# A spectral mixer and a gated FFN on one core: the head between them written in another order

## The chip, the cores and the metric

The kernel runs on one core of a Trainium2 chip. Its engines are TensorE (PE in the profile, PEld for its weight loads), VectorE (DVE), ScalarE (ACT), GpSimd (POOL) and SyncE (SP, which issues the DMAs here). Each has a queue of its own and runs it in order; an instruction that waits holds up what stands behind it on its engine. The metric is the device time of one execution in microseconds. The kernel before takes 500.88 us, the median of 3 runs (500.87 to 501.19).

## The reference

```
def _A_ref(x, w_r, w_i):                       # x: [1, 2048, 576]
    X = rfft2(x.astype(float32), axes=(-2, -1))
    X = X * (w_r + 1j * w_i)
    return irfft2(X, s=(S, D)).astype(bfloat16)

def _B_ref(x, w_gate, w_up, w_down):           # 576 -> 4608 -> 576
    return (_gelu(x @ w_gate) * (x @ w_up)) @ w_down

x = A_x
h = x + _A_ref(_layernorm(x, axis=-1), A_w_r, A_w_i)
out = h + _B_ref(_layernorm(h, axis=-1), B_w_gate, B_w_up, B_w_down)
```

Inputs and output are bfloat16. `_layernorm` subtracts a row's mean and divides by the root of its variance plus 1e-5, and `_gelu` is the tanh form.

## The kernel before

The 2048 rows lie in 16 tiles of 128 rows, `h_sb[:, h]`, and the two transforms are matrix products split into factors (16 by 128 along the rows).

**The spectral part** (to about 59 us). Rows are normalised and transformed in groups of 16 (`row16`), and then a loop runs over the eight entries of `order` = 1, 2, ... 7, 0. Iteration i does the column transform of entry i (`f2`, copied from PSUM by `f2_out`, L489), the 128-point transform of entry i - 1 (`f3`, copied at L514), VectorE's complex multiplication with the weights (`wmul`, L543 to L575) and the inverse 128-point transform of an older entry (`i3`, products at L592 and L616, copies into `EO` at L600 to L629). `EO[0]` and `EO[1]` hold the two halves x = 0 and 1 of the inverse; the last entry, 0, belongs to x = 1.

**Column products.** `inv_cols(x, g)` is the inverse column transform of half x for the pair of row tiles 2g and 2g + 1: ten matmuls into one PSUM tile (`cs_ps`, L643), then its copy. For g = 0 and 1 the copy gives two bfloat16 tiles `cs` (L666 on ScalarE, and for x = 1 one of the two at L664 on VectorE); for g of 2 and more one float32 tile `cw` on ScalarE (L656). This text calls them product (x, g) and copy (x, g).

**The head** (L843 to L867, about 60 to 73 us) brings the first four row tiles into the form that the FFN reads. `add_rows(g)` forms the inverse 16-point transform in two PSUM tiles (`y_ps`, L764, 16 matmuls), the y pair of row tiles 2g and 2g + 1. `add_sum(h)` adds one of them to `h_sb` on VectorE, with the row's sum read out behind it (L809), and has ScalarE square the result for the row's sum of squares (L817). `head_rstd(h)` makes variance and mean of it by three small VectorE instructions (L822, L825, L826) and the reciprocal root on POOL (L827). `norm_row(h)` normalises the row (L136); `turn(h)` transposes it by 18 TensorE instructions (L836) and VectorE copies the result into `hl` (L837). Tiles 0 and 1 go that way. Tiles 2 and 3 are normalised in a doubled form (`norm2`, L789) and transposed by a DMA from SP (`flip`, L801). `load_wd(2)` stands behind them on SP.

**The FFN.** `gate(t, f, ...)` computes 128 of the 4608 gate and up columns for a block of up to 512 rows: 18 matmuls into one PSUM tile (`gu`, L890), GELU on ScalarE (L898) and the multiplication on VectorE (L899), which is the last reader of the PSUM tile. Since tiles 0 and 1 are ready first, the first six gates run on 256 rows alone, and the column products that remain stand between them. After them come the main gates, 36 per block of four row tiles, with the rest of the row tiles' sums, statistics and rows put between them by a table (`todo`: `fold`, `add_both`, `stats2`, `norm2`, `flip`), and after each block the down products (`acc`, L926 and L945) and the output.

**Order and PSUM.** The whole runs under `tc.manual_schedule()`: each engine's instructions come in the order in which the text issues them. All PSUM tiles of these stages have one tag with four buffers, the whole of PSUM:

```
def two(name):
    return psum.tile([P, 2, 512], FP32, name=name, tag="two", bufs=4)
```

So a product whose tile is the fifth waits until the last reader of an earlier tile is done. In the head of before, the written order is: products (0,0) to (0,2), the last but one `i3`, (0,3), (0,4), the last `i3`, (0,5), (1,0), (1,1), both y pairs, sums 0 and 1, (0,6), sum 2, (0,7), rstd 0, sum 3, rstd 1, rows 0 and 1, (1,2), (1,3), both transposes, and rstd, row and flip of tiles 2 and 3; and products (1,4) to (1,7) stand behind the second to fifth of the six half gates.

Of the kernel before, what the change touches and what calls it, by code (L numbers as in the profile page):

```python
# [9 lines left out]
ACT = mybir.ActivationFunctionType  # L10
ALU = mybir.AluOpType
FP32 = mybir.dt.float32
# [8 lines left out]
P = 128  # L21
# [5 lines left out]
JP = J + 1  # L27
# [14 lines left out]
def kernel_body(  # L42
# [13 lines left out]
    A = nc.scalar  # L56
# [4 lines left out]
    keep = ctx.enter_context(tc.tile_pool(name="keep", bufs=1))  # L61
# [4 lines left out]
    def two(name):  # L66
        return psum.tile([P, 2, 512], FP32, name=name, tag="two", bufs=4)
# [8 lines left out]
    def const(name, val):  # L76
        t = keep.tile([P, 1], FP32, name=name)
        V.memset(t[:], val)
        return t

    zerob = const("zerob", 0.0)
# [166 lines left out]
    def angle_c(sl):  # L248
        drop_sign(ab[:, sl], ab[:, sl])
# [4 lines left out]
    def cosine(sl):  # L254
        A.activation(TF[:, sl, 1, :], ab[:, sl], ACT.Sin, bias=nhpib[:], scale=2.0 * PI / S)

    def minus_sine(sl):
        V.tensor_scalar(TF[:, sl, 0, :], TF[:, sl, 2, :], -1.0, None, op0=ALU.mult)

    def turn_tf(sl):  # L260
        nc.sync.dma_start(
            TI[:, sl].rearrange("p k r q -> p (k r) q"), TF[:, sl].rearrange("p k r q -> p (k r q)"), transpose=True
        )
# [200 lines left out]
    order = [1, 2, 3, 4, 5, 6, 7, 0]  # L464
# [6 lines left out]
    def f2(c):  # L471
        ps = two("pq_ps")
        col = slice(slot[c] * P, (slot[c] + 1) * P)
        steps = [(par, t) for par in range(2) for t in (par, par + 2, 4)]
        if c == order[0]:
            steps.sort(key=lambda s: s[1] == 4)
        for par, t in steps:
            T.matmul(  # L478
                ps[:, par, 0:JP],
                lhsT=Bt[:, t, col],  # L480
                rhs=DT[:, t // 2, par] if t < 4 else DF[:, par],
                start=(t == par),
                stop=(t == 4),
            )
        pq[c] = wk.tile([P, 2, JP], BF16, name="pq", tag="pq", bufs=6)
        pq_ps[c] = ps

    def f2_out(c, copy=A.copy, rs=slice(0, 2)):
        copy(  # L489
            pq[c][:, rs].rearrange("p r (j a) -> p r j a", a=2),  # L490
            pq_ps[c][:, :, 0:JP].rearrange("p a (r j) -> p r j a", r=2)[:, rs],
        )
# [27 lines left out]
    def sums_of(k):  # L520
        g, hs = gk[k], hk[k]
        x = xab[k] = wk.tile([P, 2, 2, JP], BF16, name="xab", tag="xab", bufs=2)
        V.tensor_tensor(x[:, 0, :, 0:J], g[:, :, 0:J], hs[:, :, 0:J], ALU.subtract)
        V.tensor_tensor(x[:, 1, ::-1, 0:J], g[:, :, 0:J], hs[:, :, 0:J], ALU.add)
# [109 lines left out]
    cs = {}  # L634
    cw = {}

    def inv_cols(x, g):

        ps = two("cs_ps")
        for w in range(NW):  # L640
            for e in range(2):
                rows = slice(64 * e, 64 * e + JW)
                T.matmul(  # L643
                    ps[:, e, 0:JP],
                    lhsT=EO[x][rows, w, 2 * g : 2 * g + 2].rearrange("p h e k l -> p (h e k l)"),
                    rhs=DQ[rows, w] if w or e else DT[rows, 0, :, 0, :],
                    start=(w == 0),
                    stop=(w == NW - 1),
                )
        pv = ps[:, :, 0:JP].rearrange("p t (q a) -> p t q a", q=2)  # L650
        if g >= 2:
            if x == 0 or g == 2:
                cw[x, g] = eop.tile([P, 2, JP], FP32, name=f"cw{x}{g}")[:]
            else:
                cw[x, g] = cwb[:, g - 3]
            A.activation(  # L656
                cw[x, g].rearrange("p t (a q) -> p t q a", q=2), pv, ACT.Copy, scale=Y_SCALE
            )
            return
        ts = [eop.tile([P, JP], BF16, name=f"cs{x}{g}{t}") for t in range(2)]  # L660
        for t in range(2):
            dst = ts[t][:].rearrange("p (a q) -> p q a", q=2)
            if x == 1 and t == 1:
                V.tensor_scalar(dst, pv[:, t], Y_SCALE, None, op0=ALU.mult)  # L664
            else:
                A.activation(dst, pv[:, t], ACT.Copy, scale=Y_SCALE)  # L666
        cs[x, g] = ts
# [4 lines left out]
    for i in range(n + 1):  # L672
        last = i >= n
        if not last:
            f2(order[i])
            if i != 1:
                f2_out(order[i])
        if i == 0:
            f2(order[0] + 8)
            for r in range(2):  # L680
                f2_out(order[0] + 8, V.tensor_copy, slice(r, r + 1))
            angle_c(rest)
            minus_sine(rest)

        if 1 <= i <= n:
            f3(order[i - 1], 0)
            f3(order[i - 1], 1)
            if i == 1:
                f2_out(order[1])
                sums_of(order[0])  # L690
            else:
                if i == 2:
                    cosine(rest)
                    turn_tf(rest)
                    pre = [load_gu(g) for g in range(3)]
                    nc.sync.dma_start(wd_a[:], wd_view[:, 0:NWA, :])
                wmul(order[i - 2], i - 1, order[i - 1])
        if not last and i:
            f2(order[i] + 8)
            f2_out(order[i] + 8)  # L700
        if i >= 3:
            for s in range(3):
                i3(order[i - 3], s)
        if last:
            wmul(order[i - 1], i)
        if i == 1:
            scr_pool.__exit__(None, None, None)
            eop = ctx.enter_context(tc.tile_pool(name="eop", bufs=1, side="right"))
            EO = [eop.tile([P, 5, H, 2, 4, 8], BF16, name=f"EO{x}", tag=f"EO{x}") for x in range(2)]
    for g in (0, 1, 2):  # L710
        inv_cols(0, g)
    for s in range(3):
        i3(order[6], s)
    for g in (3, 4):
        inv_cols(0, g)
    for s in range(3):
        i3(order[7], s)
    inv_cols(0, 5)

    spw.__exit__(None, None, None)  # L720
    spec.__exit__(None, None, None)
# [32 lines left out]
    def add_rows(g):  # L754


        ys = [two("y_ps") for _ in range(2)]
        sl = (slice(0, DH), slice(DH, 0, -1))
        for b in range(2):
            steps = [(x, t) for x in range(2) for t in range(2 if g < 2 else 1)]  # L760
            for s, (x, t) in enumerate(steps):
                for i in range(2):
                    rows = slice(64 * i, 64 * i + 64)
                    T.matmul(  # L764
                        ys[i][:, b, 0:DH],
                        lhsT=G16[rows, b * t, x, :],
                        rhs=cs[x, g][t][rows, sl[b]] if g < 2 else both[x, g][rows, b, :],
                        start=(s == 0),
                        stop=(s == len(steps) - 1),
                    )  # L770
        return ys
# [33 lines left out]
    def add_sum(h, ys, squares=True):  # L805


        hv = h_sb[:, h, :].rearrange("p (b n) -> p b n", b=2)
        V.scalar_tensor_tensor(  # L809
            hv, ys[h % 2][:, :, 0:DH], 1.0, hv, op0=ALU.mult, op1=ALU.add, accum_out=sums[:, h, 0:1]  # L810
        )
        if squares:
            sum_squares(h)
# [5 lines left out]
    def head_rstd(h):  # L819


        V.scalar_tensor_tensor(  # L822
            mv2[:, h, 1:2], sums[:, h, 0:1], sums[:, h, 0:1], sums[:, h, 1:2], op0=ALU.mult, op1=ALU.subtract
        )
        V.tensor_scalar(rstd2[:, h : h + 1], mv2[:, h, 1:2], -1.0 / (D * D), 1e-5, op0=ALU.mult, op1=ALU.add)  # L825
        V.tensor_scalar(mv2[:, h, 0:1], sums[:, h, 0:1], 1.0 / D, None, op0=ALU.mult)  # L826
        G.tensor_tensor(rstd2[:, h : h + 1], rstd2[:, h : h + 1], mhalf[:, h : h + 1], ALU.pow)  # L827

    def turn(h):


        q = h % 4 * P
        pt = psum.tile([P, 2048], BF16, name="pt", tag="two", bufs=4)
        for r in range(NR):
            for p0 in (0, 64):
                T.transpose(pt[p0 : p0 + 64, r * P : (r + 1) * P], ln2[h][:, r * 64 : (r + 1) * 64], ident[:])  # L836
        V.tensor_copy(hl[0][:, :, q : q + P], pt[:, 0 : NR * P].rearrange("p (r q) -> p r q", q=P))  # L837
# [4 lines left out]

    inv_cols(1, 0)  # L843
    inv_cols(1, 1)
    y0 = add_rows(0)
    y1 = add_rows(1)
    add_sum(0, y0)
    add_sum(1, y0)
    inv_cols(0, 6)
    add_sum(2, y1)  # L850
    inv_cols(0, 7)
    head_rstd(0)
    add_sum(3, y1)
    head_rstd(1)
    norm_row(0)
    norm_row(1)
    inv_cols(1, 2)
    inv_cols(1, 3)
    turn(0)
    turn(1)  # L860
    head_rstd(2)
    norm2(2)
    flip(2)
# [34 lines left out]
        A.activation(g_sb, gu[:, 0, 0:n], ACT.Gelu_apprx_tanh)  # L898
        V.tensor_tensor(p_sb(f)[:, lo:hi], g_sb, gu[:, 1, 0:n], ALU.mult)  # L899

    late = [(1, g) for g in range(4, 8)]
    for f in range(2 * FQ):
        gate(0, f, groups[f // FQ], f % FQ, 0, 2 * P)
        if f and late:
# [100 lines left out]
```

## Time and profile before

| | |
|---|---|
| median of 3 runs | 500.88 us |
| the profiled execution | 500.97 us |
| its span in the trace | 499.1 us |
| instructions | 12531 |
| PE busy | 488.1 us (98%) |
| DVE busy | 222.4 us (45%) |
| ACT busy | 162.7 us (33%) |
| POOL busy | 29.0 us (6%) |
| granted TensorE clock | full in all of the 40 slices |

Times are microseconds from the start of the span, mean durations nanoseconds. A row of the timeline gives start, duration, engine, line, operation, what it writes and reads, its shape, how many were merged, and in brackets the idle time of the engine ahead of it with what ended that. Merged rows overlap a little. TensorE's instructions are pipelined, so a row's end lies behind the start of the next one, and "PE busy" is not TensorE at its peak. The chain of waits is followed back from the last instruction and gives, for each stretch of time, the work that everything behind it waited for.

### The profile page before, as it was taken

The numbers are of one execution on the slowest core, as the hardware profiler recorded it, in microseconds if no ns is written. First come the engines' busy times: TensorE is split into PE (matmuls) and PEld (weight loads), VectorE is DVE, ScalarE is ACT, GpSimd is POOL, SyncE is SP. The second block draws the span as 40 slices with busy tenths as digits, with TensorE's granted clock in tenths as the row PEclk, the third lists the DMA queues.
The fourth block names the chain that finished last, engine by engine and source line by source line (L and its number), as shares of the span: only waits on it lengthen the run. The fifth ranks groups of instructions, "written<-read, shape, count | busy, mean of one in ns | idle before, by whom it ended". The sixth has DMA issues, their size and how long they took to land.

```text
span 499.1 us, 12531 instructions
## 1 busy us (share of the span) xinstructions
PE 488.1 (98%) x5606; PEld 341.8 (68%) x5608; DVE 222.4 (45%) x439; ACT 162.7 (33%) x289; POOL 29.0 (6%) x78
## 2 busy tenths in 40 slices
PE   6999989999999999999999999999999999999997
PEld 3567778555579975555599955555799655555995
DVE  8989776788641235433311245333211333333111
ACT  8989874223310112323200132332110223233000
POOL 8500010011110000000000000000000000000000
PEclk9999999999999999999999999999999999999999
DMA  9739659789960019977630069876600276760000
GB/s 289 216 62 222 192 147 246 158 171 198 175 145 13 3 49 195 207 163 159 155 75 3 1 156 209 182 159 151 143 3 1 74 159 159 157 146 1 14 13 25
DMA packets 89469, 62.33 MB, mean 125 GB/s; under 512 B 23110, under 2 KB 88006, under 8 KB 89414
## 3 DMA queue, kind: packets, MB, share of 16 engines
q1 hardware_dynamic: 89126, 60.34, 54.1%
q0 software_dynamic: 288, 1.18, 0.8%
q8 instruction: 44, 0.72, 0.6%
q14 instruction: 11, 0.09, 0.1%
HBM read 52.65 MB, written 2.36 MB: 110 GB/s over the span
## 4 chain that ended last, share of the span: by engine, by line
PE 90%; DVE 2%; ACT 1%; POOL 0%; issue 0%
PE gu L890 55%; PE acc L926 27%; PE acc L945 2%; PE eo_ps L592 2%; PE cs_ps L643 1%; PE pq_ps L478 1%; PE y_ps L764 1%; DVE h_sb L809 1%; PE gh_ps L495 0%; PE gh_ps L496 0%; POOL rstd L827 0%; PE eo_ps L616 0%; DVE hrow L789 0%; DVE Bt L837 0%; PE pt L836 0%
## 5 line engine op out<-in xcount | busy, mean ns | idle before, releaser
L890 PE MATMUL gu<-Bt,wgu 64*128 64x512 bf16 (+1 forms) x2700 | 282.4, 367 | 0.9 <-DVE mv L822 0.9
L890 PEld LDWEIGHTS <-wgu 64*128 64x128 bf16 x2700 | 159.6, 94 | 119.7 <-issue 1.1
L899 DVE TENSOR_TENSOR P_sb<-g_sb,gu 128x512 bf16<-128x512 f32 (+1 forms) x150 | 99.4, 664 | 146.0 <-ACT g_sb L898 146.0
L898 ACT ACTIVATE g_sb<-gu 128x512 f32<-128x512 f32 (+1 forms) x150 | 87.0, 580 | 194.6 <-PE gu L890 194.6
L926 PEld LDWEIGHTS <-P_sb 64*128 64x128 bf16 x2160 | 128.5, 94 | 4.5
L926 PE MATMUL acc<-wd,P_sb 64*128 64x288 bf16 x1440 | 91.0, 283 | 0.0
L935 DVE TENSOR_TENSOR part<-part,acc 128x576 f32<-128x576 f32 x15 | 11.3, 754 | 111.6 <-ACT part L934 111.6
L934 ACT COPY part<-acc 128x576 f32<-128x576 f32 x15 | 9.6, 639 | 122.8 <-PE acc L926 122.8
L926 PE MATMUL acc<-wd_a,P_sb 64*128 64x288 bf16 x720 | 46.9, 283 | 0.0
L789 DVE TENSOR_SCALAR hrow<-h_sb,mv,rstd 128x1152 bf16<-128x1152 bf16 x14 | 12.1, 868 | 1.2 <-POOL rstd L827 1.2
L478 PE MATMUL pq_ps<-DT,Bt 128*128 128x290 bf16 x64 | 12.3, 286 | 0.0
L285 PE MATMUL f2t<-h_sb,ident 128*128 128x512 bf16 x26 | 8.0, 459 | 3.7 <-DMA h_sb<-in_A_x_dram 3.6
L643 PE MATMUL cs_ps<-DQ,EO 58*128 58x290 bf16 x144 | 11.6, 283 | 0.0
L937 DVE TENSOR_TENSOR h_sb<-h_sb,part 128x576 bf16<-128x576 bf16 x15 | 11.4, 757 | 0.5
L133 POOL TENSOR_TENSOR rstd<-rstd,mhalf 128x1 f32<-128x1 f32 (+1 forms) x16 | 11.4, 714 | 1.3
L478 PEld LDWEIGHTS <-Bt 128*128 128x128 bf16 x96 | 9.2, 97 | 2.5
L297 PE MATMUL f2t<-F,xn 128*128 128x256 bf16 x64 | 9.2, 275 | 1.1 <-DVE xn L136 1.1
L643 PEld LDWEIGHTS <-EO 58*128 58x128 bf16 x160 | 8.2, 94 | 2.8 <-issue 1.1
L132 POOL TENSOR_SCALAR rstd<-mv 128x1 f32<-128x1 f32 (+1 forms) x16 | 3.9, 241 | 103.7 <-DVE mv L118 103.5
L489 ACT CAST pq<-pq_ps 128x580 bf16<-128x580 f32 x15 | 9.6, 668 | 0.0
L123 ACT ACTIVATE junk<-h_sb 128x576 bf16<-128x576 bf16 x14 | 9.4, 677 | 0.4 <-DMA h_sb<-in_A_x_dram 0.4
L117 DVE BATCH_NORM_STATS2 st<-h_sb 128x6 f32<-128x288 bf16 x21 | 9.3, 442 | 0.0
(132 smaller groups left out, 265.0 us busy)
## 6 DMA issues: line engine op xcount, KB each, us to landing
wgu<-in_B_w_gate_dram SPq DMA_DIRECT2D x48, 432.0 KB
wgu<-in_B_w_up_dram SPq DMA_DIRECT2D x48, 432.0 KB
wd<-in_B_w_down_dram SPq DMA_DIRECT2D x2, 1728.0 KB
wd_a<-in_B_w_down_dram SPq DMA_DIRECT2D x1, 1728.0 KB
out_dram<-h_sb SPq DMA_DIRECT2D x3, 576.0 KB
h_sb<-in_A_x_dram SPq DMA_DIRECT2D x4, 288.0 KB
h_sb<-in_A_x_dram SPq DMA_DIRECT2D x2, 576.0 KB
WR<-in_A_w_r_dram SPq DMA_DIRECT2D x1, 650.2 KB
```

The source lines that it names most:

```text
L133: G.tensor_tensor(dst[:, sl], dst[:, sl], mhalf[:, sl], ALU.pow)
L478: T.matmul(ps[:, par, 0:JP], lhsT=Bt[:, t, col], rhs=DT[:, t // 2, par] if t < 4 else DF[:, par], start=(t == par), stop=(t == 4),)
L592: T.matmul(pv[:, n], lhsT=z[:, a, w].rearrange("p b j -> p (b j)"), rhs=TI[:, ts[k], 1 - a : 3 - a, :], start=(a == 0), stop=(a == 1),)
L643: T.matmul(ps[:, e, 0:JP], lhsT=EO[x][rows, w, 2 * g : 2 * g + 2].rearrange("p h e k l -> p (h e k l)"), rhs=DQ[rows, w] if w or e else DT ...
L789: V.tensor_scalar(hrow[:], h_sb[:, h, :].rearrange("p (r k) -> p r k", k=64).unsqueeze(2).to_broadcast([P, NR, 2, 64]), mv2[:, h, 0:1], rs ...
L890: T.matmul(gu[:, c, 0:n], lhsT=w[rows, r, i * P : (i + 1) * P], rhs=hl[tcnk % 2][rows, r, lo:hi], start=(r == 0), stop=(r == NR - 1),)
L898: A.activation(g_sb, gu[:, 0, 0:n], ACT.Gelu_apprx_tanh)
L899: V.tensor_tensor(p_sb(f)[:, lo:hi], g_sb, gu[:, 1, 0:n], ALU.mult)
L926: T.matmul(accs[i][:, c, 0:DH], lhsT=p_sb(f)[rows, st * P : (st + 1) * P], rhs=wd[f // NWA][rows, f % NWA, c * DH : (c + 1) * DH], start=( ...
L935: V.tensor_tensor(part, part, accs[1][:, :, 0:DH], ALU.add)
L937: V.tensor_tensor(hv, hv, part, ALU.add)
L945: T.matmul(acc[:, 0, 0:DH], lhsT=p_sb(f)[:, st * P : (st + 1) * P], rhs=wd[f // NWA][:, f % NWA, cc], start=(f == 0), stop=(f == NFT - 1),)
```

## The change

Four edits to the order, and no change to what is computed.

- `inv_cols` is split into its matmuls (`inv_mm`) and its copy (`inv_out`), so that they can be issued apart.
- In the spectral loop the copy of entry order[1] (`f2_out`) is issued straight behind its product, ahead of the two `f3` copies of order[0], as for all other entries.
- Product (0,5) leaves its place ahead of the head. In the head a one-column GELU is issued on ScalarE behind the copies of (1,1), so that the GELU table is loaded there. The first y pair is followed by the products (0,5) and (0,6), then the second y pair; sums 0 and 1; the copies of (0,5) and (0,6); product (0,7); rstd 0 and 1, rows 0 and 1, the copy of (0,7), both transposes with their copies; then (1,2), sums 2 and 3, and tiles 2 and 3 as before.
- Product (1,3) leaves the head for the list that stands between the half gates, which then holds (1,3) to (1,7), behind the second to sixth.

```
+    inv_ps = {}
     def inv_cols(x, g):
-        ps = two("cs_ps")
+        inv_mm(x, g)
+        inv_out(x, g)
+
+    def inv_mm(x, g):
+        ps = inv_ps[x, g] = two("cs_ps")
         for w in range(NW):
...
-        pv = ps[:, :, 0:JP].rearrange("p t (q a) -> p t q a", q=2)
+
+    def inv_out(x, g):
+        pv = inv_ps[x, g][:, :, 0:JP].rearrange("p t (q a) -> p t q a", q=2)
...
             f2(order[i])
-            if i != 1:
-                f2_out(order[i])
+            f2_out(order[i])
...
             f3(order[i - 1], 1)
             if i == 1:
-                f2_out(order[1])
                 sums_of(order[0])
...
     for s in range(3):
         i3(order[7], s)
-    inv_cols(0, 5)
...
     inv_cols(1, 0)
     inv_cols(1, 1)
+    A.activation(keep.tile([P, 1], FP32, name="first_gelu")[:], zerob[:], ACT.Gelu_apprx_tanh)
     y0 = add_rows(0)
+    inv_mm(0, 5)
+    inv_mm(0, 6)
     y1 = add_rows(1)
     add_sum(0, y0)
     add_sum(1, y0)
-    inv_cols(0, 6)
-    add_sum(2, y1)
-    inv_cols(0, 7)
+    inv_out(0, 5)
+    inv_out(0, 6)
+    inv_mm(0, 7)
     head_rstd(0)
-    add_sum(3, y1)
     head_rstd(1)
     norm_row(0)
     norm_row(1)
-    inv_cols(1, 2)
-    inv_cols(1, 3)
+    inv_out(0, 7)
     turn(0)
     turn(1)
+    inv_cols(1, 2)
+    add_sum(2, y1)
+    add_sum(3, y1)
     head_rstd(2)
     norm2(2)
     flip(2)
...
-    late = [(1, g) for g in range(4, 8)]
+    late = [(1, g) for g in range(3, 8)]
     for f in range(2 * FQ):
         gate(0, f, groups[f // FQ], f % FQ, 0, 2 * P)
         if f and late:
```

## The prediction

> **What bounds the kernel now.** I read the page's first, second and fourth parts, then the chain of waits over the stretch that the change edits (about 59 to 77 us), then the timeline of all engines there. The page says that TensorE is busy nearly all the time and carries the chain:
>
> ```profile
> PE 488.1 (98%) x5606; PEld 341.8 (68%) x5608; DVE 222.4 (45%) x439; ACT 162.7 (33%) x289; POOL 29.0 (6%) x78
> ...
> PE 90%; DVE 2%; ACT 1%; POOL 0%; issue 0%
> ```
>
> After 74 us no wait of a matmul is listed at all, so whatever TensorE loses or gains before then passes to the end unchanged. Between 59 and 74 us the chain leaves TensorE (start, duration, engine, tile, line):
>
> ```profile
> 62.26 2.11 DVE h_sb L809 x6
> ...
> 67.07 0.71 PE pt L836 x18
> ...
> 67.80 0.76 DVE Bt L837
> 68.56 0.14 DVE mv L822
> ...
> 72.19 0.42 DVE P_sb L899
> ```
>
> That is: sums of tiles 0 to 2, the second row's transposes, its copy, and then not gate 0, whose matmuls follow at 68.71, but VectorE's rows of tiles 2 and 3, behind which the first multiply (L899) stands. The timeline shows who waits for that multiply:
>
> ```profile
> 63.05 0.68 ACT L817 ACTIVATE junk<-h_sb 128x576 bf16<-128x576 bf16 x1 [1.56 <-DVE h_sb L809]
> ...
> 65.47 0.28 PE L643 MATMUL cs_ps<-DT,EO 58*128 58x290 bf16 x1 [0.25 <-DVE h_sb L809]
> ...
> 68.14 1.28 ACT L898 ACT_TABLE_LOAD   x1
> ...
> 71.51 0.71 ACT L656 ACTIVATE cwb<-cs_ps 128x580 f32<-128x580 f32 x1 [0.24 <-PE cs_ps L643]
> ...
> 72.19 1.15 DVE L899 TENSOR_TENSOR P_sb<-g_sb,gu 128x256 bf16<-128x256 f32 x3
> ...
> 72.65 0.28 PE L643 MATMUL cs_ps<-DT,EO 58*128 58x290 bf16 x1 [0.19 <-DVE P_sb L899]
> ```
>
> There are four PSUM tiles. When TensorE came to the product (1,5) (72.65) they had held gates 0, 1, 2 and (1,4); (1,4) was copied out by 72.22, yet TensorE waited for gate 0's multiply (72.61). At 65.47 it waited likewise for tile 3's sum (65.42) though (0,6) was out at 65.09. Both tiles went to whoever comes next in the written order, not to the first one free. TensorE is idle 2.8 us between 58.90 and the end of the six half gates at 77.46 (work: 11 column products of 0.63, 32 matmuls of 0.061, 36 transposes of 0.03, 6 half gates of 0.975, together 15.75 of 18.56).
>
> **The moved column copy** (tile order[1], L489). ScalarE is idle 0.74 us ahead of the 28.00 copy, and the moved copy takes 0.63 there, so that row shifts by 0 to 0.05. TensorE's two waits of 0.26 at 30.32 and 33.60 may shrink (0.4 at most). But VectorE runs without a listed wait from here to 57.80, and the last products wait for it:
>
> ```profile
> 29.21 0.47 DVE L523 TENSOR_TENSOR xab<-g,hs 128x578 bf16<-128x578 bf16 x1 [0.80 <-ACT hs L514]
> ...
> 57.66 1.15 PEld L616 LDWEIGHTS <-Zt 128*64 128x64 bf16 x40 [0.24 <-DVE Zt L571]
> ```
>
> It starts behind the same ScalarE copy as now. Ends -0.4 and +0.05; I take 0, the VectorE row being the one that decides.
>
> **Column product (0,5) leaves its place before (1,0).** It covered the copies of the last eo tile (ends 59.23, 59.48, 59.49). Now (1,0) stands there itself and starts at 59.29 instead of 59.54: 0.25 earlier, or nothing if it waits for all three. Its copy and VectorE's copy behind it follow 0.23 earlier, so the first sum starts at 62.02 for 62.25.
>
> **GELU table on ScalarE.** Load 1.28 (row at 68.14) behind the copy of (1,1), from 61.27 to 62.55; the one-column GELU by the 128x1 accumulator read of 0.19 and the 128x256 GELU of 0.38, say 0.25: 62.80. Square 0 is wanted at 62.82 (0.04 after the sum), so the 1.56 us of idle time just cover it. Ends: 0, and +0.45 if the 0.48 us between load and GELU at 69.90 belonged to the load. I take 0: that row's wait is for the matmul.
>
> The Trainium skill ("ScalarE: Activation LUTs", What ACT_TABLE_LOAD costs) adds a drain of about 1.38 us to each load, 2.66 together. By it square 0 would be 1.3 us late and the sum below 3.0 in place of 1.7; the trace disagrees so far, with the load 0.02 us behind the copy before it and at most 0.48 ahead of the next activation.
>
> **ScalarE's order becomes the way to the second row.** The second pair of y tiles now waits for the first pair's sums (62.78, 63.46), and holds two of the four PSUM tiles until sums 2 and 3, which stand behind both row copies. So the other products share two tiles, each freed by a ScalarE copy. Rows as now (squares one per 0.68, copies 0.69, product to its end 0.81): squares 62.82 and 63.51, copy (0,5) 64.19 to 64.88, (0,6) to 65.47; product (0,7) waits for the first of these, 64.93 to 65.74, its copy 65.77 to 66.46. The first row's transposes run 65.58 to 66.27, its copy 66.31 to 67.07. The second row is normalised by 66.00 (square 1 read at 64.29, L822 to L826 0.46, rstd 0.57 to 0.73, row 0.42), but has no tile before 66.46: transposes 66.52 to 67.21, copy 67.25 to 68.01, where it is 67.80 to 68.56 now. Gain 0.55, where 1.0 would be had without the wait. Gate 0 starts at 68.13 for 68.67, with (1,2) under the copies and (1,3) still to do.
>
> **Sums 2 and 3 behind the copies.** VectorE: 68.01 less an overlap of 0.08, two sums of 0.68 (with their read), 69.37. Behind them on VectorE stand rstd and rows 2 and 3 and every multiply; on ScalarE squares 2 and 3 (68.74 to 70.20) stand ahead of GELU 0 (70.11 for 69.90, harmless). L822 of tile 2 needs square 2's read (69.51): 69.55 for 68.48. From there to the end of multiply 0 VectorE and POOL go as now (68.48 to 72.61, 4.13): 73.69, 1.08 later. POOL has nothing added. The transposing DMAs of rows 2 and 3 and the load of wd 2 behind them on SP's queue go 1.08 later; the last of these transposes is issued by 73.54 now and first needed at 77.46, wd 2 only in the acc stage from 144.76 on: nothing.
>
> **TensorE.** Gate 0 68.13, gate 1, (1,3), gate 2: 3 x 0.975 + 0.63, free at 71.68, the four tiles used. The next, (1,4), takes gate 0's by the written order: 73.73. Idle 2.05. Then four products and three half gates: 4 x 0.625 + 3 x 0.975 = 5.43, end 79.16 for 77.46. The same as idle time: 0.39 + 0.26 + 0.48 + 0.51 + 0.41 + 0.10 + 0.35 + 2.05 = 4.55 for 2.81. Sum +1.7 us.
>
> The profiled execution is 500.97 (span 499.1 and 1.9 around it), the median 500.88. 500.97 + 1.7 = 502.67; against the median 502.6, which I give.
>
> **Rivals.**
> (a) The product (1,4) takes the tile of (1,3), free at about 71.6, not gate 0's. Then it fills the gap, and gate 3 waits for multiply 0: 73.73 + 3 x 0.625 + 3 x 0.975 = 78.54, +1.08, 502.0. For it: the copy comes 2 us ahead of the multiply, a far wider gap than the 0.4 at 72.2; against it: both waits shown went by the written order.
> (b) The table costs more than its row, or squares behind it need the sine table back (another 1.28; the trace has copies behind GELU without a load, but no square). The chain from square 0 to the second row moves by 1.3: 503.9. Against it: the 0.48 us above.
> (c) The second row's transposes get the first row's tile (copied by 67.07) instead of (0,7)'s: 0.6 later throughout, 503.2. Against it: the written order.
> (d) Not slower: VectorE takes the first multiplies ahead of rows 2 and 3, so that the 2.05 us wait is not there. Idle 2.5 for 2.81, -0.3: 500.6. It decides from multiply 0 ending by 71.6. For it: GELU 0 is done by 70.5. Against it: VectorE ran rows and multiplies exactly as written before, and no gate was let ahead.
>
> **How the numbers follow.** A measurement of this kernel tells some 0.2% (1.0 us, runs 500.87 to 501.19) from no change. Chances: forecast 0.52, (a) 0.24, (b) 0.08, (c) 0.07, (d) 0.09. The unknowns move forecast and (a) by +0.25 (eo copies), +0.45 (load) and -0.4 (column copy). Range 501.7 to 503.6: it holds nearly all of the forecast, (a) and (c), and leaves out (b) and (d). Slower by over 0.2% is above 501.88: forecast, (b), (c), and 0.6 of (a): 0.81. Within 0.2%: the rest of (a) and 0.06 of (d): 0.16. Faster: 0.03, (d) with the gain of the column copy.
>
> **What would show it.** Right: a table load at 61.3 with no square late; the second y pair and (0,7) waiting for L809 and L656; the second row's transposes waiting for (0,7)'s copy, not for L136; multiply 0 at about 73.3; one TensorE wait of 2 us for L899 at (1,4). Wrong: that wait at gate 3 (a), square 0 well past 62.9 or a second load (b), transposes behind L837 (c), multiplies ahead of the second L789 (d). If TensorE reaches 58.90's work earlier than now, the column copy was mispriced.

## The result, and the profile after

The changed kernel takes 502.60 us, the median of 8 runs, against 500.98 us for 8 runs of the kernel before beside it: 1.0039 times as long, with an interval of 1.0028 to 1.0050. (The medians alone give 1.0032; the ratio takes in the spread, among it one execution of 504.45 and one of 503.45.) The profiled execution took 502.58 us (span 500.8) for 500.97 (499.1), so 1.6 us longer. In a second set of four runs beside the kernel before it came to 1.0046 (1.0030 to 1.0061; one of the four, at 504.37, had a lower TensorE clock, see the last section), and its profiled execution to 502.60:

> The changed kernel once more beside it on the same chip: 1.6 to 1.7 us above the kernel before and 2.0 above the version with the wide rows behind; if the 2 us wait of TensorE sometimes lowers its granted clock, some executions 1 to 2 us above the rest.

All line numbers below the column products are shifted in the new kernel: the sums are L814 (L809 before), the squares L822 (817), the first variance instruction L827 (822), the wide rows L794 (789), the transposes and their copies L841 and L842 (836, 837), the gates L899 (890), the multiplies L908 (899), a column product L649 (643) and its float32 copy L664 (656). In the experiments' kernels they move by a few more.

The page's first part, and the chain by engine from its fourth, show TensorE as the bound as before, with 2% of the span less of the chain on it:

```profile
PE 488.9 (98%) x5606; PEld 340.0 (68%) x5608; DVE 222.8 (44%) x439; ACT 163.2 (33%) x290; POOL 29.2 (6%) x78
...
PE 88%; ACT 3%; DVE 1%; issue 1%; POOL 0%
```

The chain of waits over the head (start, duration, engine, tile, line) shows where those 2% are. It now leaves TensorE from the first sum at 62.05 to the product (1,4) at 73.73, except for (0,7), (1,2) and one row of transposes:

```profile
62.84 1.46 ACT junk L822 x4
...
65.75 0.70 ACT cw L664
...
66.50 0.69 PE pt L841 x18
...
68.75 0.79 ACT junk L822 x2
...
73.27 0.42 DVE P_sb L908
...
73.73 0.80 PE cs_ps L649 x10
```

There are two stretches. From 62 to 68 ScalarE's squares and copies set when the second row can be turned; from 68.7 to 73.7 the squares of tiles 2 and 3, their statistics and their wide rows set when VectorE comes to the first multiply. The timeline (start, duration, engine, line, operation, tiles and shapes, and in brackets the wait and what ended it) has the instructions that the prediction dated, here the table load, square 0, the second row's transposes, the second wide row, the first multiplies and (1,4):

```profile
61.29 1.28 ACT L850 ACT_TABLE_LOAD   x1
...
62.84 0.68 ACT L822 ACTIVATE junk<-h_sb 128x576 bf16<-128x576 bf16 x1
...
66.50 0.69 PE L841 MATMUL pt<-ident,hflat 128*64 128x128 bf16 x18 [0.16 <-ACT cw L664]
...
72.48 0.87 DVE L794 TENSOR_SCALAR hrow<-h_sb,mv,rstd 128x1152 bf16<-128x1152 bf16 x1 [0.60 <-POOL rstd L832]
73.27 1.07 DVE L908 TENSOR_TENSOR P_sb<-g_sb,gu 128x256 bf16<-128x256 f32 x3
...
73.73 0.28 PE L649 MATMUL cs_ps<-DT,EO 58*128 58x290 bf16 x1 [1.94 <-DVE P_sb L908]
```

The last row is the loss: TensorE stands 1.94 us at (1,4) because that product's PSUM tile is gate 0's, and gate 0's multiply stands on VectorE behind the wide rows, the second of which ends at 73.35.

**A measure for the runs that follow.** VectorE's first `xab` (L523) starts between 29.21 and 29.79 in the executions here, in kernels that differ up to there in nothing but the place of the moved column copy. Part of that is when the input rows arrive: in the latest of them ScalarE stands 0.40 us for rows of the input at 6.85, which it does not in the profiled execution of the changed kernel. All that follows is shifted with it. So the comparisons of single profiled executions go from that start to the first matmul of the third y pair (`y_ps<-both`), which stands behind all half gates:

| | L523 | third y pair | between | against before |
|---|---|---|---|---|
| before | 29.21 | 82.38 | 53.17 | |
| after | 29.23 | 84.09 | 54.86 | +1.69 |
| after, second set | 29.24 | 84.12 | 54.88 | +1.71 |

### The profile page after: what moved, and what is told of

Same layout as the page of the kernel before. It is cut to its first block, busy times and chain, and to the rows that moved or that the text cites. A ratio compares the mean times of both kernels' runs of the same rounds, so it can differ in the third digit from the quotient of the medians.

```text
span 500.8 us, 12531 instructions
## 1 busy us (share of the span) xinstructions
PE 488.9 (98%) x5606; PEld 340.0 (68%) x5608; DVE 222.8 (44%) x439; ACT 163.2 (33%) x290; POOL 29.2 (6%) x78
## 4 chain that ended last, share of the span: by engine, by line
PE 88%; ACT 3%; DVE 1%; issue 1%; POOL 0%
PE gu L899 55%; PE acc L935 26%; PE acc L954 2%; PE pq_ps L478 1%; PE eo_ps L592 1%; PE cs_ps L649 1%; PE y_ps L769 1%; ACT cw L664 1%; ACT junk L822 0%; ACT EO L600 0%; PE gh_ps L496 0%; PE gh_ps L495 0%; ACT cs L674 0%; POOL rstd L832 0%; ACT xab L507 0%
## 5 line engine op out<-in xcount | busy, mean ns | idle before, releaser
L899 PE MATMUL gu<-Bt,wgu 64*128 64x512 bf16 (+1 forms) x2700 | 282.6, 367 | 0.1
L899 PEld LDWEIGHTS <-wgu 64*128 64x128 bf16 x2700 | 158.6, 94 | 120.0 <-issue 0.3
L908 DVE TENSOR_TENSOR P_sb<-g_sb,gu 128x512 bf16<-128x512 f32 (+1 forms) x150 | 99.4, 664 | 146.6 <-ACT g_sb L907 146.6
L794 DVE TENSOR_SCALAR hrow<-h_sb,mv,rstd 128x1152 bf16<-128x1152 bf16 x14 | 12.2, 868 | 1.2 <-POOL rstd L832 1.2
L649 PE MATMUL cs_ps<-DQ,EO 58*128 58x290 bf16 x144 | 11.9, 283 | 0.0
L649 PEld LDWEIGHTS <-EO 58*128 58x128 bf16 x160 | 8.2, 94 | 4.8 <-issue 2.9
```

The source lines that it names most:

```text
L649: T.matmul(ps[:, e, 0:JP], lhsT=EO[x][rows, w, 2 * g : 2 * g + 2].rearrange("p h e k l -> p (h e k l)"), rhs=DQ[rows, w] if w or e else DT ...
L794: V.tensor_scalar(hrow[:], h_sb[:, h, :].rearrange("p (r k) -> p r k", k=64).unsqueeze(2).to_broadcast([P, NR, 2, 64]), mv2[:, h, 0:1], rs ...
L899: T.matmul(gu[:, c, 0:n], lhsT=w[rows, r, i * P : (i + 1) * P], rhs=hl[tcnk % 2][rows, r, lo:hi], start=(r == 0), stop=(r == NR - 1),)
```

## Experiments: what was priced at nothing

Theory: the moved column copy is worth nothing, the early table load is hidden, and the whole 1.7 us comes from VectorE's order around multiply 0. The rivals are a table load that costs more than its row, a column copy that gives something back, and for the big term the tile that (1,4) gets.

**The column copy in its old place.** The rest of the change stays.

```
-            f2_out(order[i])
+            if i != 1:
+                f2_out(order[i])
...
             if i == 1:
+                f2_out(order[1])
                 sums_of(order[0])
```

> The changed kernel with the one column copy of order[1] back in its old place. Theory (VectorE sets the pace of the spectral loop): the copy's place is worth nothing; the last products of that loop stay where they are within 0.05 us, and so does the profiled time, 502.6. Rival (TensorE's waits for that copy count): up to 0.4 us more, 503.0.

Measured: 503.14 us in one profiled execution, which looks like a loss of 0.5. It isn't one. L523 started 0.56 us later in this execution (29.79 for 29.23), and everything behind it is shifted by just that: 84.65 - 29.79 = 54.86, the same as after. The first `i3` in the timeline of the changed kernel, and the VectorE row whose `Zt` it reads, are

```profile
34.91 0.46 DVE L530 TENSOR_TENSOR Zt<-zb,za 128x580 bf16<-128x580 bf16 x1
...
35.47 1.25 PE L592 MATMUL eo_ps<-TI,Zt 128*128 128x256 bf16 x10 [0.48 <-ACT hs L514]
```

and in that of the kernel with the copy back:

```profile
36.02 1.25 PE L592 MATMUL eo_ps<-TI,Zt 128*128 128x256 bf16 x10
```

With the copy early, TensorE gets through its products sooner and then waits 0.48 us for the first `i3`; with the copy late it comes to the same `i3` without a wait. In both, `i3` starts 6.23 to 6.24 us behind L523 (6.24 in the kernel before as well). The bracket names a ScalarE copy, but the last `hs` copy ahead of it had ended at 35.02; what ends last there is VectorE's `Zt`, at 35.37. So VectorE's row sets it, as the prediction had it; the copy is worth 0.00.

**No early GELU.**

```
-    A.activation(keep.tile([P, 1], FP32, name="first_gelu")[:], zerob[:], ACT.Gelu_apprx_tanh)
```

> The changed kernel without the one-column GELU. Theory: the table load falls in front of GELU 0, 70.1 to 71.4, and GELU 0 and 1 are done by 72.2, still ahead of multiply 0's turn on VectorE at 73.3: no change, 502.6. Rival (the early load is worth its 1.28 us): 503.9.

Measured: 502.82 us in one execution, with L523 at 29.46; between the two marks 54.87, +1.70 to before. The load goes back to its old place behind gate 0 (70.45 to 71.73) and nothing moves, which this kernel's timeline shows:

```profile
71.75 0.66 ACT L906 ACTIVATE g_sb<-gu 128x256 f32<-128x256 f32 x2
...
73.51 1.07 DVE L907 TENSOR_TENSOR P_sb<-g_sb,gu 128x256 bf16<-128x256 f32 x3
...
73.97 0.28 PE L649 MATMUL cs_ps<-DT,EO 58*128 58x290 bf16 x1 [1.95 <-DVE P_sb L907]
```

GELU 0 starts 1.6 us later than with the early table (71.75 for 70.11, of which 0.23 is this execution's later start), and the multiply doesn't feel it, since the wide rows hold it until 73.5. The early table costs nothing and, in this order, brings nothing.

**Two loads more.** Behind `first_gelu` come a one-column sine and another one-column GELU, whose results nobody reads. It prices a table load where the cover of 1.56 us is used up.

```
+    A.activation(keep.tile([P, 1], FP32, name="one_sine")[:], zerob[:], ACT.Sin)
+    A.activation(keep.tile([P, 1], FP32, name="next_gelu")[:], zerob[:], ACT.Gelu_apprx_tanh)
```

> The changed kernel with a one-column sine and another one-column GELU behind the first, so that three table loads stand ahead of square 0 instead of one. Theory (the load fits its gap with nothing to spare, and ScalarE's chain from square 0 carries gate 0 and the squares of tiles 2 and 3): square 0 moves by two loads of 1.28 and two activations of 0.20, 2.95 in all, and the time by as much: 505.5. Rival (ScalarE has slack before the second row): 503 to 504. By the Trainium skill (ScalarE: Activation LUTs, What ACT_TABLE_LOAD costs), which adds a drain of about 1.38 us to each load, it would be about 508.3.

Measured: 506.24 us in one execution. Its timeline, the ScalarE rows and the second row's transposes:

```profile
61.28 1.28 ACT L850 ACT_TABLE_LOAD   x1
62.57 0.20 ACT L850 ACTIVATE first_gelu<-zerob 128x1 f32<-128x1 f32 x1
62.78 1.28 ACT L851 ACT_TABLE_LOAD   x1
...
65.58 0.20 ACT L852 ACTIVATE next_gelu<-zerob 128x1 f32<-128x1 f32 x1
65.69 0.67 ACT L822 ACTIVATE junk<-h_sb 128x576 bf16<-128x576 bf16 x1
...
69.31 1.17 PE L841 MATMUL pt<-ident,hflat 128*64 128x128 bf16 x18 [0.16 <-ACT cw L664]
```

Each load is a row of 1.28 us, starts 0.01 us behind the activation before it and is followed by the next activation 0.01 to 0.02 us after its end. Square 0 went from 62.84 to 65.69: 2.85 us for two loads and two activations, where the cover left 0.06. So rival (b) falls by its price as well as by its place: here a load costs its row and no more. By the Trainium skill ("ScalarE: Activation LUTs", What ACT_TABLE_LOAD costs), which adds a drain of about 1.38 us to each load, the same two would by estimate have taken 2.8 us longer still; no row here shows such a drain. The third y pair came 3.66 us later than after's; 2.85 of it is the chain, and the rest came with a lower TensorE clock, which the last section tells: the second row's transposes take 1.17 us here and 0.69 in the changed kernel.

## Experiments: which tile (1,4) gets, and where the wait falls

**(1,4) takes the tile of (1,3).** This is rival (a) made true.

```
-        ps = inv_ps[x, g] = two("cs_ps")
+        ps = inv_ps[x, g] = inv_ps[1, 3] if (x, g) == (1, 4) else two("cs_ps")
```

> The changed kernel in which product (1,4) is written into the PSUM tile of (1,3) instead of gate 0's. Theory (which tile is handed out decides 0.6 us of the 1.7): (1,4) starts at 71.7, gate 3 then waits for multiply 0 until 73.7, the main gates start 0.63 earlier; 501.95. Rival (TensorE is held by something else than that tile): no change, 502.6.

Measured: 502.14 us, median of 10 runs, 1.0021 times before (1.0012 to 1.0031); between the marks 54.23, +1.06. In its timeline (1,4) starts without a wait, and gate 3 stands instead:

```profile
71.86 0.28 PE L649 MATMUL cs_ps<-DT,EO 58*128 58x290 bf16 x1
...
73.96 1.16 PE L899 MATMUL gu<-Bt,wgu 64*128 64x256 bf16 x18 [1.29 <-DVE P_sb L908]
```

Rival (a) was priced at +1.08. The gap between it and the forecast, 0.63, is just one column product, which either fills the wait or stands behind it.

**The copy of (1,3) written ahead of multiplies 0 and 1.** The prediction said that tiles go "by the written order". Here `gate` hands back its multiplication for f of 0 and 1, and both are issued behind the copy of (1,3). VectorE and ScalarE each keep their own order; only the order of the text between them changes, so that the tile of (1,3) is given back first in the text.

```
+        def times():
+            V.tensor_tensor(p_sb(f)[:, lo:hi], g_sb, gu[:, 1, 0:n], ALU.mult)
+
+        if tcnk == 0 and f < 2 and lo == 0:
+            return times
+        times()
...
+        waiting.append(gate(0, f, groups[f // FQ], f % FQ, 0, 2 * P))
         if f and late:
             inv_cols(*late.pop(0))
+        if f == 1:
+            for times in waiting:
+                times()
```

> The changed kernel with the copy of (1,3) written ahead of the multiplies of gates 0 and 1, each engine's own order being the same. The prediction's wording (the tile goes by the written order): (1,4) would take the tile of (1,3) and the time would be 501.95, as with the shared tile. Rival (tiles are dealt by another rule): (1,4) still waits for multiply 0 until 73.7, 502.6. In the program as built (1,4) has gate 0's tile still, so the rival is expected.

Measured: 502.59 us in one execution, between the marks 54.87, +1.70. Its timeline still has the wait in the same place:

```profile
73.74 0.28 PE L649 MATMUL cs_ps<-DT,EO 58*128 58x290 bf16 x1 [1.95 <-DVE P_sb L910]
```

So the tile isn't chosen by which last reader is written first. That it was gate 0's and not that of (1,3) was right; the rule given for it isn't shown by this run. What does choose it stays open. Going simply round the four buffers is not it, since by that the second row's transposes of the changed kernel would wait for the second y pair, and they go at 66.50, ahead of its sums. The tile that was asked for longest ago, among those whose last reader is already written, agrees with the waits shown of before, after and here, but no run was made to tell that from other rules.

**Product (1,3) back in the head.** Its matmuls go ahead of gate 0, behind (1,2), and its copy behind sum 3, so the half gates have four products between them as before.

```
     inv_cols(1, 2)
+    inv_mm(1, 3)
     add_sum(2, y1)
     add_sum(3, y1)
+    inv_out(1, 3)
...
-    late = [(1, g) for g in range(3, 8)]
+    late = [(1, g) for g in range(4, 8)]
```

> The changed kernel with product (1,3) back ahead of gate 0 (its copy behind square 3) and (1,4) to (1,7) between the half gates as before. Theory: gate 0 starts 0.6 later (68.7), but it and the gates behind it end before multiply 0 as ever; multiply 0 stays at 73.3 to 73.7, and behind it stands one product less, 0.63: 501.95. Rival (moving (1,3) was free, or filled a gap well): 502.6, or more by the 0.6 that gate 0 is late, 503.2.

Measured: 502.18 us, median of 10, 1.0023 (1.0014 to 1.0033); between the marks 54.23, +1.06. Two rows of its timeline:

```profile
68.82 2.14 PE L901 MATMUL gu<-Bt,wgu 64*128 64x256 bf16 x36
...
73.84 0.28 PE L649 MATMUL cs_ps<-DT,EO 58*128 58x290 bf16 x1 [1.27 <-DVE P_sb L910]
```

Gate 0 starts 0.8 us later than after's 68.04 (0.12 of it this execution's later start), and the end comes 0.63 earlier. The time at which VectorE comes to multiply 0 hardly moves, and work put ahead of the wait is work that doesn't stand behind it. What the change bought by starting gate 0 sooner was idle time of TensorE a little later.

## Experiments: taking the wait away

**Wide rows behind multiplies 0 and 1.** The statistics of tiles 2 and 3 stay in the head; their wide rows and transposing DMAs, and the load behind them, go behind the second half gate. This is rival (d) made true.

```
     head_rstd(2)
-    norm2(2)
-    flip(2)
     head_rstd(3)
-    norm2(3)
-    flip(3)
-    load_wd(2)
...
         if f and late:
             inv_cols(*late.pop(0))
+        if f == 1:
+            norm2(2)
+            flip(2)
+            norm2(3)
+            flip(3)
+            load_wd(2)
```

> The changed kernel with the wide rows of tiles 2 and 3 and their transposing DMAs (L794, L806) issued behind the multiplies of gates 0 and 1; the small statistics of both tiles stay ahead. Theory (the loss is the wait for multiply 0, which stands behind sums 2 and 3 and both wide rows): multiply 0 ends at 71.1 instead of 73.7, (1,4) starts at 71.7 without a wait, the main gates at 77.1 instead of 79.2; 500.5, below the kernel before by 0.35. Rival (the loss lies ahead of gate 0, in the y pair that holds two of four PSUM tiles): no change, 502.6. A second rival (the rows' DMAs then come too late for the main gates): a new wait of TensorE for Bt near 77, and 500.5 plus that wait.

Measured: 500.73 us, median of 10 runs, 0.9997 times before (0.9988 to 1.0007); between the marks 52.75, -0.42. The timeline:

```profile
70.84 0.74 DVE L903 TENSOR_TENSOR P_sb<-g_sb,gu 128x256 bf16<-128x256 f32 x2
71.50 1.65 DVE L794 TENSOR_SCALAR hrow<-h_sb,mv,rstd 128x1152 bf16<-128x1152 bf16 x2
...
71.82 0.29 PE L649 MATMUL cs_ps<-DT,EO 58*128 58x290 bf16 x1
```

Multiply 0 stands 2.4 us earlier, (1,4) starts without any wait, and behind it no wait of TensorE is listed up to the main gates. This is the run that carries the verdict: with the wait gone, the 1.7 us are gone, and all the rest of the change is still there. One of the ten executions took 502.87 at a full clock; it was not the profiled one, and why it was longer stays open. Once more, to see whether what is left is a gain over before:

> The version with the wide rows behind multiplies 0 and 1 once more, for an interval. Theory: in its trace the main gates start 0.41 us earlier, counted from the first sum of the spectral loop, than in the kernel before; 0.4 us less than before, ratio 0.9992, at the edge of what five rounds tell. Rival (some executions lose more than that to a new wait): no difference or more than before.

Measured: 500.70 us, median of 11, 0.9996 (0.9987 to 1.0005); between the marks 52.87, -0.30. The profiled executions gain 0.3 to 0.4 us, as rival (d) had it (-0.3); by the times alone this order can't be told from the kernel before. The kernel before was not run with its own wide rows moved likewise. The wait for multiply 0 in its trace is 0.19 us (at 72.65), so some of the 0.3 to 0.4 may be had without the rest of the change.

**The second y pair behind the transposes.** In the changed kernel the second pair holds two PSUM tiles from 63.5 until sums 2 and 3, and the second row's transposes wait for a tile until 66.50. Here the pair is formed behind the transposes.

```
-    y1 = add_rows(1)
     add_sum(0, y0)
...
     turn(1)
+    y1 = add_rows(1)
     inv_cols(1, 2)
```

> The changed kernel with only the second y pair moved, to behind both transposed rows. Theory: product (0,7) no longer waits for a ScalarE copy and the second row's transposes start behind its normalisation (65.9 instead of 66.5), its copy ends at 67.4 instead of 68.0; but the 16 matmuls of the pair now lie between that and gate 0, and sums 2 and 3 still stand ahead of multiply 0: multiply 0 within 0.15 us of where it was, 502.6. Rival (the hold on PSUM tiles was the price): 0.5 us less, 502.1.

Measured: 503.55 us, median of four, 1.0049 (1.0033 to 1.0065). Two of the four were 502.73; the other two had a lower TensorE clock (last section). The head did what was expected of it:

```profile
65.96 1.42 DVE L842 COPY Bt<-pt 128x1152 bf16<-128x1152 bf16 x2
...
67.69 0.76 DVE L814 SCALAR_TENSOR_TENSOR h_sb<-y_ps,h_sb 128x576 bf16<-128x576 f32 x1 [0.30 <-PE y_ps L769]
...
68.32 0.70 ACT L664 ACTIVATE cw<-cs_ps 128x580 f32<-128x580 f32 x1 [2.33 <-PE cs_ps L649]
...
68.90 0.67 ACT L822 ACTIVATE junk<-h_sb 128x576 bf16<-128x576 bf16 x1
...
73.87 0.28 PE L649 MATMUL cs_ps<-DT,EO 58*128 58x290 bf16 x1 [2.01 <-DVE P_sb L908]
```

The second row's copy ends at 67.38 for 67.99, so the missing tile costs 0.61; the prediction had 0.45 for it (a gain of 0.55 where 1.0 could be had). But (1,4) starts at 73.87 for 73.73. Sum 2 does come sooner, at 67.69 for 67.90; its square does not, at 68.90 for 68.75, because on ScalarE it stands behind copy (1,2), which starts at 68.32 for 68.02, since product (1,2) now follows the y pair. The statistics, the wide rows and multiply 0 follow the square, so here the faster second row buys only more idle time.

**Both together, with all products that fit ahead of the gates.** Pair 2 behind the transposes, (0,7), (1,2) and (1,3) in the tiles that it leaves free, and the wide rows behind multiplies 0 and 1.

```
-    y1 = add_rows(1)
     add_sum(0, y0)
     add_sum(1, y0)
+    inv_mm(0, 7)
+    inv_mm(1, 2)
     inv_out(0, 5)
     inv_out(0, 6)
-    inv_mm(0, 7)
+    inv_mm(1, 3)
...
     inv_out(0, 7)
+    inv_out(1, 2)
+    inv_out(1, 3)
     turn(0)
     turn(1)
-    inv_cols(1, 2)
+    y1 = add_rows(1)
     add_sum(2, y1)
     add_sum(3, y1)
...
+        if f == 1:
+            norm2(2)
+            flip(2)
+            norm2(3)
+            flip(3)
+            load_wd(2)
```

> A version for gain: the changed kernel's start, but the second y pair is formed only behind both transposed rows, products (0,7), (1,2) and (1,3) go ahead of them, and the wide rows of tiles 2 and 3 stand behind the multiplies of gates 0 and 1. Theory (the loss came from the y pair's hold on PSUM tiles and from the work ahead of multiply 0): second row's copy done at 67.8, gate 0 at 68.0 with only (1,4) to (1,7) left, multiply 0 at 71.4, no wait of TensorE behind gate 0, main gates 1.0 to 1.1 us ahead of the kernel before; about 499.9. Rival (the wide rows' DMAs are too late for the main gates): a wait for Bt at 76 to 77 that eats up to the whole gain, 500 to 501.

Measured: 501.66 us, median of 12, 1.0026 (1.0011 to 1.0040); in the profiled execution 53.13 between the marks, -0.04. That is a miss: faster was expected, it is slower. The half gates did end earlier, gate 5 at 76.7, and then the main gates stood for the transposing DMAs, which is what the rival said; its timeline shows it:

```profile
71.89 1.65 DVE L794 TENSOR_SCALAR hrow<-h_sb,mv,rstd 128x1152 bf16<-128x1152 bf16 x2
...
72.79 2.68 SPq L806 DMA_TRANSPOSE Bt<-hrow  x2
...
77.67 2.58 PE L897 MATMUL gu<-Bt,wgu 64*128 64x256 bf16 x44 [0.70 <-DMA Bt<-hrow]
```

The second wide row was done at 73.54, and TensorE was released at 77.67, 4.1 us later. The head's gain was 1.0 us (76.7 for 77.46 in the kernel before, in an execution that started 0.24 later), and the wait took all of it back. So between the marks the profiled execution is no slower than before; the loss of the median is in the others, which spread from 500.84 to 504.27. Part of that is the clock (last section), and what else the slower ones lose one trace can't show.

**Eight half gates.** The same with two half gates more (their second halves then run as half blocks later) to cover the transfer, and the load of wd 2 moved on to the fourth group of gates.

```
-    for f in range(2 * FQ):
+    NH = 2 * FQ + 2
+    for f in range(NH):
...
+            if tcnk == 0 and gi == 3:
+                load_wd(2)
```

> The version with the late y pair, with eight half gates instead of six ahead of the main gates (the last two from the third weight group) and the load of wd 2 issued behind the sixth weight group. Theory (the gain of about 1.0 was there and was eaten by the wait for the transposing DMAs of tiles 2 and 3, which land at 77.7): the main gates start at 78.7 without a wait, with 1.96 us more of the gates' work already done, 1.0 us ahead of the kernel before; 499.9. Rival (the third weight group is held too long and the fourth comes late): a wait for wgu between 84 and 90, 500 to 501.

Measured: 501.69 us, median of 11, 1.0014 (1.0005 to 1.0023). Slower again, by less. The profiled execution was the fastest of the eleven (500.99). Its half gates reach on to 78.7, and still a wait for the transposed rows is left, and one of the weight loads, at 89.82, waits 0.64 us for the weights themselves, which is the wait that the rival named. One row of the timeline, one of the chain of waits, and one of the waits of TensorE's weight loads (in all, times, longest):

```profile
79.01 5.09 PE L897 MATMUL gu<-Bt,wgu 64*128 64x256 bf16 x90 [0.29 <-DMA Bt<-hrow]
```

```profile
73.96 4.91 DMA Bt<-hrow
```

```profile
PEld L897 <- DMA wgu<-in_B_w_up_dram: 0.6, 1, 0.6
```

The transposed rows came later than in the version with six half gates: by the chains of waits their transfers end at 78.87 here and at 77.53 there, though the second wide row was done sooner, at 73.32 for 73.54. So the cover of two half gates was sized on a duration that did not hold, and why it was longer wasn't tried. That eight half gates use up the gate and up weights sooner than they arrive is the likely reason for the second wait, but it wasn't tried by itself. None of the versions here beats the kernel before by more than can be measured.

## Why the prediction was right

The time (502.6 predicted, 502.60 measured) came out by the steps given for it, nearly all within 0.1 us. That the two agree to 0.01 is luck: the steps sum to 1.74 us, which the prediction rounded to 1.7, the marks measure 1.69 to 1.71, and the profiled executions as a whole differ by 1.61.

- **Column copy, 0.** Right, and for the reason given: `i3` starts 6.23 to 6.24 us behind L523 in all three orders. (Of the two waits of TensorE that the prediction read as 0.26, the second is 0.23 in the trace; the term was put at 0 and does not rest on it.)
- **(0,5) leaves, 0.25 gained.** (1,0) at 59.27 for 59.29 predicted, the first sum at 62.03 for 62.02.
- **GELU table, 0.** The load at 61.29 to 62.57, square 0 at 62.84 for 62.82. The drain by which the Trainium skill ("ScalarE: Activation LUTs", What ACT_TABLE_LOAD costs) would have made it 1.3 late isn't there, in this kernel or behind the two loads more. That squares and copies need no load back shows in the single load of the head's timeline.
- **ScalarE's chain to the second row.** (0,7) at 64.91 for 64.93, behind the first copy; second transposes at 66.50 for 66.52, behind the copy of (0,7); VectorE's copy ends at 67.99 for 68.01, 0.57 sooner than before (0.55 predicted). Rival (c), the first row's tile, falls by the row at 66.50. The experiment with the pair behind the transposes shows that the two tiles held by the second pair are what costs time there, 0.61 where the prediction had 0.45.
- **Sums 2 and 3 behind the copies, 1.08 on multiply 0.** Square 2 at 68.75 for 68.74, the first variance instruction at 69.56 for 69.55, multiply 0's end at 73.69 for 73.69. No run put sums 2 and 3 alone back ahead of the row copies; that the 1.08 is theirs rests on these rows.
- **TensorE's wait at (1,4).** (1,4) at 73.73 as predicted, and the half gates ended at 79.18 for 79.16. The bracket's 1.94 is counted from the end of gate 2's row (71.78), the prediction's 2.05 from where the next matmul could start. Counted as the prediction does (70.62 and 0.975 for the gate), the wait was 2.13, since gate 0 started 0.09 sooner, at 68.04: that gain was idle time at (1,4).

One reason isn't borne out: that (1,4) takes gate 0's tile because tiles go by the written order. With the order of the last readers turned round in the text, (1,4) still took gate 0's. The choice between forecast and rival (a), worth 0.63 us, was right on waits seen before and not on that rule.

Rival (d) didn't come about by itself: multiply 0 stood behind the second wide row, as written. Its price was right, though (-0.3). With the wide rows written behind the first multiplies, the same head takes 0.3 to 0.4 us less than before in its profiled executions.

## What to carry to other kernels

When work is moved ahead on one row of tiles, look at what stands behind it on each in-order engine: here the first gate started 0.7 us sooner, and the multiplies that give back the PSUM tiles stood 1.1 us later, behind rows that nobody needed until 79 us. A head that feeds a saturated engine is judged at the first wait of that engine behind it, and filling work belongs ahead of that wait. Before single profiled executions are compared within 1 us, measure between two marks in the kernel, since what lies ahead of the first mark alone moved the end by up to 0.56 us between two kernels that do the same work there.

## What the runs showed of the hardware

**In some executions the TensorE clock halves for 3.4 us, in both traces that have it behind a wait of TensorE of 2 to 3 us.** In the stretches of the profiled execution with the pair behind the transposes (stretch, sum, then busy time and instructions of PE, PEld, DVE, ACT and POOL, the granted clock, DMA share and GB/s), the mean clock falls from 1.00 to 0.67 behind TensorE's wait of 2.01 us (to 73.87) and is full again from 79:

```profile
73.80:79.00 5.20, 5.13 (x61) 4.41 (x62) 1.10 (x4) 1.81 (x4) 0.00 (x0) 0.67 1.05 210
79.00:84.00 5.00, 5.00 (x94) 4.91 (x90) 1.69 (x5) 2.87 (x6) 0.00 (x0) 1.00 0.67 220
```

In steps of 0.3 us the clock is 1.00 up to 74.8, 0.50 in every step from 75.1 to 78.1 and 1.00 from 78.4: half the clock for some 3.4 us, beginning about 1.1 us behind the wait. By estimate it costs 5.20 x 0.33 = 1.7 us, as much as the whole change: that execution took 504.37 where others of the kernel took 502.73. With two loads more the wait was 3.06 us (to 67.72), and the mean clock 0.68 and 0.75 over the six us from 68:

```profile
68.00:71.00 3.00, 2.84 (x52) 2.12 (x48) 1.69 (x4) 0.95 (x2) 0.18 (x1) 0.68 0.00 0
71.00:74.00 3.00, 3.00 (x44) 2.30 (x42) 2.06 (x8) 2.16 (x6) 0.30 (x1) 0.75 0.02 5
```

In steps of 0.4 us it is 0.50 in every step from 69.4 to 72.2 and 1.00 before 69.0 and from 72.6, again some 3.4 us.

Executions with a mean clock of 0.997 or less came in 2 of the 12 runs of the changed kernel (wait 1.94), 2 of 4 with the pair behind the transposes (2.01) and the one with two loads more; in the first two kernels they are 1.6 to 2.1 us longer than the median of the others. The three single executions of kernels with a wait of 1.95 (the copy in its old place, no early GELU, the copy of (1,3) written ahead) had a full clock. There were none in 20 runs of the two kernels whose longest wait is 1.3 us, in 21 of the kernel without the wait, or in the 71 of the kernel before that ran beside the experiments. But the order with both changes had 3 of 12, though its profiled execution, at full clock, shows no wait of TensorE over 0.7 us in or behind the head. So a wait of 2 us is not shown to be needed, and what lowers the clock there stays open. The Trainium skill ("TensorE: Matmul & The Clock Gate", What's actually happening) has the clock fall after at least one idle window of about 3.4 us; the two waits here, with the clock at half behind them, were shorter, 2.01 and 3.06, and whether other short waits filled up the window wasn't tried.

**From a wide row to TensorE, a small transposing DMA took 4.1 us in one execution and 5.7 in another.** It is 4.1 us from the end of the second row in the order with both changes (73.54 to 77.67) and 5.7 with eight half gates (73.32 to 79.01), with two rows of 128 by 1152 and 2.68 us of SyncE's queue for the two issues in both. What makes the difference wasn't tried; one thing that differs is that the load of wd 2 stands behind the two issues in the first order and not in the second. In the kernel before and after, the half gates hide it; in the order with both changes it was the bound.
